# Loading wq as four loads of every fourth partition, in a one-token attention and MLP kernel

## The chip, the cores and the metric

The kernel runs on one core of a Trainium2 chip. The core has five instruction streams: TensorE (PE), VectorE (DVE), ScalarE (ACT), GpSimd (POOL) and SyncE (SP). SP computes nothing; it issues transfers (DMAs), which sixteen DMA engines carry out. The metric is device time in microseconds of one execution. Streams are ordered among themselves by semaphores only: an instruction raises one when it is done, another waits until it has reached a value. A DMA raises its semaphore by 16 when all of its data has landed.

## The reference

One token of width 1024 goes through attention over a window of cached keys and values, and through an MLP; both results are added to the token.

```
xn  = layernorm(x)                                   # x: 1 x 1024
q   = xn @ wq                                        # wq: 1024 x 4096, 32 heads of 128
k,v = last 4096 positions of the caches              # 4 kv heads, each serves 8 q heads
o   = softmax(q k^T / sqrt(128)) v
h   = gelu(layernorm(xn) @ w1 + b1)                  # w1: 1024 x 3584
out = x + o @ wo + h @ w2 + b2                       # wo: 4096 x 1024, w2: 3584 x 1024
```

All arrays are bfloat16. Of work there is little; of weights and cache there are 39.8 MB: wq 8.4, K 4.2, V 4.2, w1 7.3, w2 7.3, wo 8.4.

## The kernel before, in words

Each large array is spread over the 128 partitions of SBUF, so that one partition holds a run of consecutive rows of the weights. For wq that is 8 rows of 4096 numbers: partition p holds rows 8p to 8p+7, which stand in one piece of 64 KB in memory, and in one piece in the tile `WA`.

The order of the loads is written out by hand, in the order in which SP issues them:

- wq into `WA` at the very start (L167, through `load_rows`, whose `dma_start` is L158), one load with semaphore `s_wq[0]`;
- after POOL has built its constants (L200), K into `KT` (L201), w1 into `W1` (L202) and V into `V` (L203), all without a further wait;
- w2 into `WA`, over wq, when the q product is done (L272 and L273);
- wo in six loads into `W1` and `KT`, over w1 and K, when the h product is done (L374 to L379);
- at the end the output (L519).

ACT issues three small loads on a queue of its own: x (L183), b1 (L184), b2 (L238).

On the engines: DVE transposes x and normalizes it with the help of one small matmul (L234 to L253), which gives `XNTb`; a second normalization gives `YTb` for the MLP. PE then forms the q product in `wide_product` (L274 to L287): it waits once for each chunk of weights, here for the single chunk of wq, and runs 64 matmuls of 512 columns (L282). q is brought into the shape that the scores need (L295 to L319). DVE transposes K in place in four parts (L324), PE computes scores (L335), DVE and ACT the softmax (L342 to L370). PE computes the h product with w1 by the same `wide_product` (L373), then the product with V (L426), then the output products with w2 and wo (L456, L463), adding x and b2 on the way. Two additions (L516) and the output's load end the kernel.

Of the kernel before, what the change touches and what calls it, by code (L numbers as in the profile page):

```python
# [19 lines left out]
NQ = 4096  # L20
# [4 lines left out]
WQ_CHUNKS = [8]  # L25
# [22 lines left out]
def bass_parallel_sum__sliding_block_cached__mixer_channel_mlp__decode_kernel(  # L48
# [18 lines left out]
    pe, dve, act, pool, sp = nc.tensor, nc.vector, nc.scalar, nc.gpsimd, nc.sync  # L67

    def sems(name, n):
        return [nc.alloc_semaphore(f"{name}{i}") for i in range(n)]  # L70

    s_x, s_b1, s_b2, s_out = (nc.alloc_semaphore(n) for n in ("s_x", "s_b1", "s_b2", "s_out"))
    s_wq = sems("s_wq", len(WQ_CHUNKS))
# [11 lines left out]
    def sb(name, shape, d):  # L85
        return nc.alloc_sbuf_tensor(name, shape, d)

    f32, bf16 = dt.float32, dt.bfloat16
    WA = sb("WA", [128, KC * NQ], bf16)
# [57 lines left out]
    wq_p = A_wq.rearrange("(p r) n -> p r n", r=KC)  # L147
# [8 lines left out]
    def load_rows(dst, src, chunks, width, semaphores, first=0, c0=0, off=0):  # L156
        for j, n in enumerate(chunks):
            sp.dma_start(  # L158
                dst[:, off + c0 * width: off + (c0 + n) * width].rearrange("p (c n) -> p c n", c=n),
                src[:, first + c0: first + c0 + n, :],  # L160
            ).then_inc(semaphores[j], 16)
            c0 += n
# [1 line left out]
    def load_cache(dst, src, sem):  # L164
        sp.dma_start(dst[:, :], src[0, :, SK - W:SK, :].rearrange("g (m b) d -> m g (b d)", m=32)).then_inc(sem, 16)

    load_rows(WA, wq_p, WQ_CHUNKS, NQ, s_wq)  # L167
    def d(ins):
        return DVE.mark(ins)

# [103 lines left out]
    def wide_product(weights, chunks, width, semaphores, vec, n, banks, name):  # L274
        k = 0
        for j, rows in enumerate(chunks):
            pe.wait_ge(semaphores[j], 16)
            for _ in range(rows):
                for b in range(2):
                    for a in range(4):  # L280
                        lo = k * width + (2 * a + b) * n
                        last = pe.matmul(  # L282
                            PS[32 * a:32 * a + 32, banks[b] * 512: banks[b] * 512 + n],
                            lhsT=vec[:, k:k + 1].to_broadcast([128, 32]), rhs=weights[:, lo:lo + n],
                            start=(k == 0), stop=(k == KC - 1))
                k += 1
        C[name] = PE.mark(last)  # L287

    wide_product(WA, WQ_CHUNKS, NQ, s_wq, XNTb, 512, [4, 5], "q")

    sp.wait_ge(PE.sem, C["q"])
# [79 lines left out]

    pe.wait_ge(ACT.sem, C["exp0"])
    wide_product(W1, W1_CHUNKS, F, s_w1, YTb, QW // 2, [4, 5], "h")  # L373
    sp.wait_ge(PE.sem, C["h"])  # L374
    load_rows(W1, wo_p, WO_CHUNKS[:2], D, s_wo[:2])
# [101 lines left out]
    for a in range(4):  # L477
        q = a % 2
# [25 lines left out]
    for a in range(4):  # L504
        q = a // 2
# [45 lines left out]
```

## Time and profile before

| | us |
|---|---|
| median of three runs | 101.5 (101.06 to 101.81) |
| the profiled execution | 100.91 |
| its span, first to last instruction | 99.5 |
| PE, DVE, ACT, POOL busy | 53.7, 42.0, 10.6, 6.4 |
| moved by DMA | 39.89 MB, 401 GB/s over the span |
| wq: issue to landing | 0.81 to 22.8 |
| K: issue to landing | 5.47 to 32.45 |
| w2: issue to landing | 27.79 to 77.3 |
| wo's largest load: issue to landing | 63.9 to 87.1 |

The profile is one execution, a little shorter than the median run. In its lines L282 is line 282 of the kernel; `out<-in` names the tiles; SPq and ACTq are instructions that issue a DMA. The time of such an instruction is the time to issue, not to move the data; the time to landing stands apart. A line of the timeline is: start, duration, engine, line, operation, tiles, and in brackets how long the engine had been idle and what released it. The chain that ended last is followed back from the last instruction, at each step to what released it. A load in the chain counts from its issue, with all of the time in which it stood in a queue. In the slices each digit is the busy share of one fortieth of the span, in tenths.

### The profile page before, as it was taken

The page shows a single profiled execution, that of the slowest core. Times are in us where ns is not written, and L with a number is a line of the kernel's source. Part 1 is how long each engine was busy: PE and PEld are TensorE (multiplying, and loading weights), DVE is VectorE, ACT ScalarE, POOL GpSimd, SP SyncE. Part 2 cuts the span into 40 slices and gives each one's busy share as a digit, 9 for nine tenths or more (in the row PEclk, how much of TensorE's full clock was granted, in tenths as well). Part 3 has the DMA queues.
Part 4 walks back from the last instruction along what each step waited for, and adds up shares of the span by engine and source line. Part 5 has one row for each costly group of instructions (what it writes and reads, how often), then busy time and mean ns, then how long its engine had stood idle before and what let it go on. Part 6 is the DMA issues. An engine that isn't in the chain of part 4 may idle for free.

```text
span 99.5 us, 859 instructions
## 1 busy us (share of the span) xinstructions
PE 53.7 (54%) x355; PEld 20.0 (20%) x355; DVE 42.0 (42%) x49; ACT 10.6 (11%) x21; POOL 6.4 (6%) x26
## 2 busy tenths in 40 slices
PE   0000220008912019999690359709999299997770
PEld 0000220003400002222120224204344033442220
DVE  0000443000073999999999202999600620000022
ACT  0000336000022000000000297000000000000030
POOL 6773000000000000000000000000000000000000
PEclk9999999999999555557999755885579957999999
DMA  9399999959999888998699999998889999999920
GB/s 369 158 448 448 503 528 422 448 250 435 421 421 580 369 369 369 484 622 352 273 435 474 421 451 392 484 599 369 369 369 431 421 421 415 412 430 387 394 90 1
DMA packets 1622, 39.89 MB, mean 401 GB/s; under 512 B 200, under 2 KB 468, under 8 KB 596
## 3 DMA queue, kind: packets, MB, share of 16 engines
q1 hardware_dynamic: 1596, 39.85, 93.7%
q8 instruction: 2, 0.03, 0.1%
q10 hardware_dynamic: 24, 0.01, 0.0%
HBM read 39.86 MB, written 0.00 MB: 401 GB/s over the span
## 4 chain that ended last, share of the span: by engine, by line
DMA 58%; DVE 22%; PE 10%; POOL 4%; ACT 2%; issue 2%; SPq 1%; POOLq 0%; DVEq 0%
DMA KT<-in_A_wo_dram 31%; DMA KT<-in_A_k_cache_dram 27%; DVE KT L324 18%; PE PS L282 6%; DVE MX L344 2%; PE PS L335 2%; ACT WA L366 1%; PE PS L456 1%; POOL B1R L180 1%; DVE BULK L509 1%; ACT Q L348 1%; SPq L158 1%; PE PS L360 1%; POOL QB L189 1%; DVE ORow L516 0%
## 5 line engine op out<-in xcount | busy, mean ns | idle before, releaser
L324 DVE STREAM_TRANSPOSE KT<-KT 128x4096 bf16<-128x4096 bf16 x4 | 17.4, 4415 | 1.3 <-DMA KT<-in_A_k_cache_dram 1.3
L335 PE MATMUL PS<-KT,QB 128*128 128x512 bf16 x32 | 11.7, 504 | 6.4 <-DVE KT L324 6.4
L426 PE MATMUL PS<-V,WA 128*128 128x512 bf16 x32 | 9.7, 479 | 0.0
L282 PE MATMUL PS<-WA,XNTb 128*32 128x512 bf16 x64 | 4.9, 478 | 8.0 <-DMA WA<-in_A_wq_dram 8.0
L456 PE MATMUL PS<-WA,GT 128*1 128x512 bf16 x56 | 7.9, 451 | 0.0
L509 DVE COPY BULK<-PS 1x256 f32<-1x256 f32 x2 | 0.8, 414 | 15.6 <-PE PS L456 15.5
L245 PE MATMUL PS<-XT,onesf 128*128 128x16 f32 x2 | 0.6, 384 | 11.5 <-DVE XT L242 11.5
L456 PE MATMUL PS<-W,OT 128*1 128x512 bf16 x50 | 5.7, 379 | 1.1 <-DMA W<-in_A_wo_dram 1.1
L282 PE MATMUL PS<-W,YTb 128*32 128x448 bf16 x64 | 5.5, 530 | 1.5 <-ACT WA L366 1.5
L295 DVE CAST Q<-PS 128x512 bf16<-128x512 f32 x1 | 0.7, 692 | 11.7 <-PE PS L282 11.7
L335 PEld LDWEIGHTS PS<-KT,QB 128*128 128x128 bf16 x32 | 3.0, 113 | 12.2 <-DVE KT L324 7.5
L234 DVE STREAM_TRANSPOSE XT<-XB 128x256 bf16<-128x256 bf16 x1 | 0.6, 626 | 10.4 <-DMA XB<-in_A_x_dram 10.4
L426 PEld LDWEIGHTS PS<-V,WA 128*128 128x128 bf16 x32 | 3.7, 119 | 5.6 <-issue 3.5
L370 DVE STREAM_TRANSPOSE WA<-WA 128x4096 bf16<-128x4096 bf16 x1 | 4.4, 4434 | 0.0
L331 PE MATMUL PS<-MRow,ML 4*128 4x512 bf16 x8 | 3.8, 469 | 0.7 <-DVE QB L317 0.7
L282 PEld LDWEIGHTS PS<-WA,XNTb 128*32 128x32 bf16 x64 | 1.9, 118 | 10.6 <-DMA WA<-in_A_wq_dram 8.2
L366 ACT ACTIVATE WA<-PS,NMB 128x1024 bf16<-128x1024 f32 (+2 forms) x3 | 3.7, 1252 | 1.8 <-DVE NMB L362 1.8
L456 PEld LDWEIGHTS PS<-WA,GT 128*1 128x1 bf16 x56 | 2.8, 96 | 4.7 <-issue 2.5
L511 ACT ACTIVATE BULK<-PS 1x256 f32<-1x256 f32 x2 | 0.7, 374 | 25.5 <-PE PS L456 25.4
L434 DVE TENSOR_TENSOR HW<-PS,MG 128x512 f32<-128x512 f32 x1 | 0.7, 692 | 6.0 <-PE PS L426 6.0
L282 PEld LDWEIGHTS PS<-W,YTb 128*32 128x32 bf16 x64 | 2.3, 138 | 4.3 <-issue 2.5
L348 ACT ACTIVATE Q<-PS 128x512 f32<-128x512 f32 x1 | 0.6, 597 | 23.5 <-DVE MX L344 23.5
(98 smaller groups left out, 42.0 us busy)
## 6 DMA issues: line engine op xcount, KB each, us to landing
W<-in_B_w_dram SPq DMA_DIRECT2D x1, 7168.0 KB, 44.5
WA<-in_B_w_dram SPq DMA_DIRECT2D x1, 7168.0 KB, 49.5
KT<-in_A_k_cache_dram SPq DMA_DIRECT2D x1, 4096.0 KB, 27.0
V<-in_A_v_cache_dram SPq DMA_DIRECT2D x1, 4096.0 KB, 53.6
W<-in_A_wo_dram SPq DMA_DIRECT2D x1, 4096.0 KB, 23.2
W<-in_A_wo_dram SPq DMA_DIRECT2D x1, 2304.0 KB, 28.3
KT<-in_A_wo_dram SPq DMA_DIRECT2D x1, 1024.0 KB, 30.4
KT<-in_A_wo_dram SPq DMA_DIRECT2D x1, 512.0 KB, 31.2
```

What stands on the lines that cost most here:

```text
L158: sp.dma_start(dst[:, off + c0 * width: off + (c0 + n) * width].rearrange("p (c n) -> p c n", c=n), src[:, first + c0: first + c0 + n, :], ...
L282: last = pe.matmul(PS[32 * a:32 * a + 32, banks[b] * 512: banks[b] * 512 + n], lhsT=vec[:, k:k + 1].to_broadcast([128, 32]), rhs=weights[: ...
L324: C["kt"].append(d(dve.transpose(KT[:, j * W:(j + 1) * W], KT[:, j * W:(j + 1) * W])))
L331: pe.matmul(bank(nb), lhsT=ML[:, :], rhs=MRow[:, :].unsqueeze(1).to_broadcast([4, 16, 32]), start=True, stop=False)
L335: last = pe.matmul(bank(nb), lhsT=QB[:, c * 128:(c + 1) * 128], rhs=kg[:, c, 16 * nb:16 * nb + 16, :], start=False, stop=(c == 3))
L344: C["mx1"] = d(dve.tensor_reduce(out=MX[:, 1:2], in_=PS[:, 2048:4096], axis=AX.X, op=ALU.max))
L348: C["s7"] = ACT.mark(act.activation(out=S7, in_=bank(7), func=ACTF.Copy))
L366: C[f"exp{j}"] = C["exp"] = ACT.mark(act.activation(out=PT[:, lo:lo + n], in_=src, func=ACTF.Exp, bias=NMB[:, 0:1], scale=SCALE, accum_out ...
L370: C["PT"] = d(dve.transpose(PT, PT))
L426: last = pe.matmul(bank(3), lhsT=PT[:, t * 128:(t + 1) * 128], rhs=V[:, t * 512:(t + 1) * 512], start=(t == 0), stop=(t == 31))
L456: ins = pe.matmul(PS[32 * q:32 * q + 1, 6 * 512:7 * 512], lhsT=vec[:, c:c + 1], rhs=row[:, :, q * 256:(q + 1) * 256], start=first, stop=last)
L509: d(dve.tensor_copy(dst, src))
```

## The change

wq comes in four loads. Load i takes the partitions i, i+4, i+8 and so on, 32 of them with their 64 KB each, and all four raise the same semaphore. PE waits for the sum of the four, 64, ahead of the q product; for the h product it waits for 16 as before. Nothing else differs; the lines of the changed kernel stand one further down.

```
-    load_rows(WA, wq_p, WQ_CHUNKS, NQ, s_wq)
+    for i in range(4):
+        sp.dma_start(WA[i:128:4, :], wq_p[i:128:4, :, :].rearrange("p r n -> p (r n)")).then_inc(s_wq[0], 16)
...
-            pe.wait_ge(semaphores[j], 16)
+            pe.wait_ge(semaphores[j], 64 if name == "q" else 16)
```

## The prediction

> **What bounds the kernel now.** I read the chain that ended last first, in order of time. Its two long pieces are waits for a transfer:
>
> ```profile
> 5.47 26.98 DMA KT<-in_A_k_cache_dram
> 32.47 17.44 DVE KT L324 x4
> ...
> 64.73 30.41 DMA KT<-in_A_wo_dram
> 95.14 0.04 issue
> 95.19 1.05 PE PS L456 x8
> ```
>
> A load of 1 MB that takes 30.41 us is not moving for 30 us; it stands in a queue. So the next view is the page's slices, with the queues:
>
> ```profile
> DMA  9399999959999888998699999998889999999920
> ...
> DMA packets 1622, 39.89 MB, mean 401 GB/s; under 512 B 200, under 2 KB 468, under 8 KB 596
> ...
> q1 hardware_dynamic: 1596, 39.85, 93.7%
> ```
>
> SP's queue, q1, carries all but some hundredths of a MB and fills 93.7% of the sixteen DMA engines' span. The two weak slices (a 3 and a 5) are no idle time: a packet is booked where it starts, and wq's packets are 64 KB. The packet records of the trace show each engine taking eight packets of 64 KB for wq, the first starting between 1.82 and 2.69 us, each later one in 2.42 us and right behind the one before it; the eighth ends between 21.8 and 22.4 us. From there to the last weights no engine pauses, apart from two fetches of instructions of about 1 us, each on a single engine.
>
> Next, SP's own instructions, to see who can delay that stream:
>
> ```profile
> 0.81 0.38 SPq L158 DMA_DIRECT2D WA<-in_A_wq_dram  x1
> 5.47 0.63 SPq L165 DMA_DIRECT2D KT<-in_A_k_cache_dram  x1
> 6.14 0.58 SPq L158 DMA_DIRECT2D W<-in_B_w_dram  x1
> 6.77 0.55 SPq L165 DMA_DIRECT2D V<-in_A_v_cache_dram  x1
> 27.79 0.34 SPq L158 DMA_DIRECT2D WA<-in_B_w_dram  x1
> 63.89 0.80 SPq L158 DMA_DIRECT2D W<-in_A_wo_dram  x2
> ```
>
> Landing is issue plus the page's time to landing. K lands at 32.45, w1 at 50.6, V at 60.4, w2 at 77.3, and the chain's last load at 95.14. w2 is issued at 27.79, 32 us before the queue in front of it is empty (V's landing). wo is issued at 63.89, 13 us before w2 has landed. So neither the q product nor the score and softmax chain decides the end: **a change of wq counts by how much it shifts the DMA stream**, and compute has 13 us to spare against it.
>
> Last, what waits for wq itself:
>
> ```profile
> 10.45 0.63 DVE L234 STREAM_TRANSPOSE XT<-XB 128x256 bf16<-128x256 bf16 x1 [10.45 <-DMA XB<-in_A_x_dram]
> 13.37 0.29 DVE L253 TENSOR_SCALAR XNTb<-XT,msx 128x8 bf16<-128x8 f32 x1
> 22.81 4.93 PE L282 MATMUL PS<-WA,XNTb 128*32 128x512 bf16 x64 [8.04 <-DMA WA<-in_A_wq_dram]
> ```
>
> The normalized x is ready at 13.66 us; the q product starts at 22.81, when the whole of wq is there.
>
> **The change part by part.** The sum is made against the profiled execution: 100.91 us, of which 99.5 are span and 1.4 lie around it. The three runs shown have a median of 101.5, 0.6 above it, so what comes out is put on that median.
>
> *The wait (L277, 64 in place of 16).* Still one wait ahead of the first matmul, for all of wq. No matmul may start early and none is held longer; queued behind it on PE is the same q product. Cost 0.
>
> *What moves.* The same 128 rows of 64 KB, 8.4 MB. Load i takes rows i, i+4, ..., two rows for each of 16 engines if the rows are dealt out evenly. Whether they are dealt so that sixteen engines still run side by side isn't shown for 32 rows. The nearest rows are the K and V loads: the outermost dimension of their source counts 32 too (m in L165), and their 32 KB packets took 1.213 us, which is 27.0 GB/s an engine, as for wq (64 KB in 2.42 us, 27.1). I take 0; the other end is the third rival.
>
> *The issue.* One instruction becomes four. A load of 128 plain rows took SP 0.34 to 0.43 us (0.38 for wq); loads of other shapes took 0.50 to 0.68 (b2 0.50, V 0.55, K 0.63, out 0.68). I take 0.55 for a load of every fourth partition, by V, which also stands behind other loads. Four take 2.2 us, 0.81 to about 3.0. K is held at 5.47 by POOL's constants (SP waits 4.5 us for them), so K, w1 and V leave when they did. If POOL's cover were gone, K would leave some 1.8 us later and still have 16 us of wq in front of it. The engines need the second load only after two packets each, at about 6.7 us, when all four are issued. So only the first issue counts: first packets come 1.01 us after wq's issue starts, 0.63 after it ends; 0.55 in place of 0.38 shifts them by **+0.17** (bounds: 0.34 gives -0.04, 0.68 gives +0.30).
>
> *The start of the engines.* First packets start over 0.87 us and mostly take about 3.0, not 2.42. If that comes from 128 rows being written out for sixteen engines, 32 rows would go quicker. If all sixteen started at 1.82 and ran at once at full rate, first packets would end at 4.24 in place of a typical 5.11: **-0.87**. But two engines that start at 1.82 and 2.37 end their first packet together at 4.86; ends don't follow starts. I take a small share, -0.1, and keep 0 and -0.87 as ends.
>
> *The seams.* There are three more ends of a load. One seam is in the trace: wq's last packet, a 4-byte semaphore write of 0.009 us, then K's first packet; K's landing is 9.68 us behind wq's, and eight packets of 1.213 us are 9.70. A seam costs about 0.01, three **+0.03** (upper end: the full latency of an isolated load, out's 1.7 us from issue to landing, three times, 5.1).
>
> [...]
>
> *The x load.* x, b1 and b2 go by ACT's queue, and the packet records show x's 512 bytes waiting for wq's second packet to end. Three more loads at SP while ACT issues x (2.06, 1.07 us long) may hold x back by a packet or two, 2.42 us each. The 9.1 us between 13.66 and 22.81 hide up to three; without that cover the q product would slip, and the 13 us of wo's issue are behind it. Cost 0.
>
> Sum: +0.17 - 0.1 + 0.03 = +0.1. **101.0 for the profiled execution, 101.6 on the median.** By the bounds of the first two terms the sum lies between -0.9 and +0.4.
>
> **The rivals.**
> 1. *An earlier start.* The small first load reaches the engines sooner and the slow first packets go: down to -0.9 us, 100.6, and more if the issue gets shorter too. For it: the 0.87 us spread. Against it: the ends that don't follow the starts, and a first issue of another shape.
> 2. *The seams cost (slower).* Engines drain at each end of a load before they go on. Place: three seams, at two packets' distance; price 0.35 us each if the next packet waits until the last one's semaphore has arrived (21.8 to 22.16 in the records), +1.1, to 5.1 by a full latency: 102.6 to 106.6. It decides as soon as a seam is over 0.35. Against it: the seam from wq to K.
> [...]
>
> [...]
>
> **How the numbers follow.** About 1% (1.0 us) is what a measurement of this kernel can tell from no change; the three runs alone span 0.75. Chances: the forecast 0.72; rival 1 0.12 (two thirds of it over 1%); rival 2 0.09; rival 3 0.07. That gives faster 0.08, same 0.76, slower 0.16. The range leaves out rival 3, most of rival 2 and the far part of rival 1: from 100.6 (the bound of -0.9) to 102.6 (a seam of 0.35).
>
> **What would show it.** In the changed profile: four issues on SP of about 0.55 us from 0.81, K's still at 5.47. wq's last landing and the start of the q product at 22.8 within half a microsecond; K 9.7 us behind; the chain again ending in a wo load that waits in the queue. Right steps with a wrong size: the q product's start and the end move by the same amount. Rival 1: both earlier by 0.5 to 1. Rival 2: wq 1 to 5 us later with packets still of 2.42 us. [...] Wrong altogether: an end that moves while K's landing doesn't.

## The result, and the profile after

The changed kernel takes 101.33 us (median of 22 runs, 101.03 to 101.98) against 100.84 before (22 runs): the ratio is 1.0054, with a 95% interval of 1.0039 to 1.007. That is half a microsecond more: real, and inside the 1% that the prediction called no change. Forecast was +0.1 us; 0.39 to 0.71 us are measured. Ratios and mean spans here and below leave out the few runs that were over 1.5% above the fastest of their kernel. The forecast time, 101.6 us, lies nearer to 101.33 than its terms deserve, and that is luck: it stood on a median of three runs, 101.5, which is 0.66 us above that of 22 runs, and this made up for the 0.39 us by which the sum fell short.

The timeline of SP's queue after, to hold against the one before (start, duration, issue):

```profile
0.81 2.72 SPq L168 DMA_DIRECT2D WA<-in_A_wq_dram  x4
5.45 0.58 SPq L165 DMA_DIRECT2D KT<-in_A_k_cache_dram  x1
6.09 0.61 SPq L158 DMA_DIRECT2D W<-in_B_w_dram  x1
6.74 0.55 SPq L165 DMA_DIRECT2D V<-in_A_v_cache_dram  x1
28.77 0.33 SPq L158 DMA_DIRECT2D WA<-in_B_w_dram  x1
65.85 0.81 SPq L158 DMA_DIRECT2D W<-in_A_wo_dram  x2
```

One issue of 0.38 us has become four, 2.72 us from the first to the last; the trace's records of the single ones give 0.58, 0.57, 0.59 and 0.84. K, w1 and V still leave at 5.45 to 6.74, behind POOL's constants. The timeline of the engines shows what became of x and of the q product:

```profile
8.65 0.63 DVE L235 STREAM_TRANSPOSE XT<-XB 128x256 bf16<-128x256 bf16 x1 [8.65 <-DMA XB<-in_A_x_dram]
11.57 0.29 DVE L254 TENSOR_SCALAR XNTb<-XT,msx 128x8 bf16<-128x8 f32 x1
23.16 5.56 PE L283 MATMUL PS<-WA,XNTb 128*32 128x512 bf16 x64 [10.20 <-DMA WA<-in_A_wq_dram]
```

x is there 1.80 us earlier (8.65 in place of 10.45), and that buys nothing: the q product waits for wq as before, 10.2 us now, and starts 0.35 later (23.16 in place of 22.81). The chain that ended last, its long pieces:

```profile
5.45 27.39 DMA KT<-in_A_k_cache_dram
32.87 17.43 DVE KT L325 x4
...
66.70 28.81 DMA KT<-in_A_wo_dram
95.51 0.04 issue
95.56 1.04 PE PS L457 x8
```

K lands 0.40 us later (32.85, before 32.45), the 1 MB load of wo 0.37 later (95.51, before 95.14), and the span is 0.4 longer. In this pair of profiles the offset that wq picks up at the start runs through the whole stream and comes out at the end nearly unchanged (0.35, 0.40, 0.37). On the way wo is issued 1.96 us later (65.85 in place of 63.89), mostly because the score matmuls behind K's last part took 4.2 us in place of 2.3, at a granted clock of 0.52 of full speed in place of 1.00. Its landing doesn't move with it: wo only waits a little less in the queue (28.81 in place of 30.41). That is the 13 us of cover, seen at work.

Where the offset comes from stands in the packet records, read for the sixteen first packets of wq in both traces:

| | before | after |
|---|---|---|
| first issue, start and duration | 0.81, 0.38 | 0.81, 0.58 |
| first packet starts at | 1.82 | 2.17 |
| from the end of the issue to it | 0.63 | 0.78 |
| sixteen first packets, median duration | 3.06 | 3.22 |
| the other 112 packets, median | 2.42 | 2.42 |
| wq landed | 22.77 | 23.12 |

### The profile page after: what moved, and what is told of

The parts are those of the page before. It is cut to its first block, busy times and chain, and to the rows that moved or that the text cites. A ratio compares the mean times of both kernels' runs of the same rounds, so it can differ in the third digit from the quotient of the medians.

```text
span 99.9 us, 862 instructions
## 1 busy us (share of the span) xinstructions
PE 53.8 (54%) x355; PEld 19.9 (20%) x355; DVE 42.0 (42%) x49; ACT 10.6 (11%) x21; POOL 6.4 (6%) x26
## 4 chain that ended last, share of the span: by engine, by line
DMA 56%; DVE 22%; PE 12%; POOL 4%; ACT 2%; issue 2%; SPq 1%; POOLq 0%; DVEq 0%
DMA KT<-in_A_wo_dram 29%; DMA KT<-in_A_k_cache_dram 27%; DVE KT L325 17%; PE PS L283 5%; PE PS L336 4%; DVE MX L345 2%; ACT WA L367 1%; PE PS L457 1%; POOL B1R L181 1%; DVE BULK L510 1%; ACT Q L349 1%; SPq L158 1%; PE PS L361 1%; PE PS L332 1%; POOL QB L190 1%
## 5 line engine op out<-in xcount | busy, mean ns | idle before, releaser
L283 PE MATMUL PS<-WA,XNTb 128*32 128x512 bf16 x64 | 5.6, 524 | 10.2 <-DMA WA<-in_A_wq_dram 10.2
L345 DVE TENSOR_REDUCE MX<-PS 128x1 f32<-128x2048 f32 x1 | 2.3, 2292 | 2.0 <-PE PS L336 2.0
```

Source lines behind the costliest of these rows:

```text
L283: last = pe.matmul(PS[32 * a:32 * a + 32, banks[b] * 512: banks[b] * 512 + n], lhsT=vec[:, k:k + 1].to_broadcast([128, 32]), rhs=weights[: ...
L345: C["mx1"] = d(dve.tensor_reduce(out=MX[:, 1:2], in_=PS[:, 2048:4096], axis=AX.X, op=ALU.max))
```

## The experiments

The theory after these two traces: a load of every fourth partition is handed over in a more general form than a plain load of 128 rows; its issue is longer by 0.20 us, its first packet follows 0.15 us later still, and as nothing else is in the queue at that moment all sixteen engines stand idle for 0.35 us more. The rival: it is the four loads, with their seams or their small shares of two rows an engine. Ratios below are to the kernel before on the same chip, with 95% intervals.

**One load, general form.** A switch of the builder keeps the load off the short form; rows, partitions and the number of loads stay.

```
+    nc.dge_precook = False
     load_rows(WA, wq_p, WQ_CHUNKS, NQ, s_wq)
+    nc.dge_precook = True
```

> One load of all 128 partitions as in the kernel before, but handed to SP in the general form that loads of other shapes take, not in the short form of a plain load of 128 rows. Theory (the form of the first issue is the whole cost): issue of wq 0.6 to 0.7 us in place of 0.38, first packets and wq's landing 0.3 to 0.4 us later, time like the changed kernel's, ratio 1.003 to 1.006. Rival (it is the four loads, by their seams or by the small share of an engine in each): issue of another length but the time of the kernel before, ratio 1.000 within 0.0015.

Measured: 101.23 us, ratio 1.0042 (1.0011 to 1.0072), and on SP's queue:

```profile
0.81 0.58 SPq L158 DMA_DIRECT2D WA<-in_A_wq_dram  x1
5.47 0.57 SPq L165 DMA_DIRECT2D KT<-in_A_k_cache_dram  x1
```

The issue takes 0.58 as in the changed kernel (0.38 without the switch), the first packet starts at 2.17 as there, and in the runs the loss is there with a single load: the interval leaves out a ratio of 1. The profile alone would not have shown it. Expected were a landing of wq 0.3 to 0.4 us later and an issue of at least 0.6; wq landed only 0.17 later than before (22.94), because the last of its first packets ended only 0.16 later (5.64, before 5.48), and the profile's span is 99.55 us, before 99.52.

**Four plain loads.** Two of each partition's eight rows in each load, all 128 partitions, one wait for 64.

```
-    load_rows(WA, wq_p, WQ_CHUNKS, NQ, s_wq)
+    load_rows(WA, wq_p, [2, 2, 2, 2], NQ, s_wq * 4)
```

> Four loads of two rows of wq each, all 128 partitions, 16 KB a partition, plain shape, one wait for 64. Theory (form of the first issue): wq's first issue 0.35 to 0.4 us, time of the kernel before, ratio 1.000 within 0.0015; wq's landing at 22.8 within 0.15. Rival (seams): three seams as in the changed kernel, ratio 1.003 to 1.006.

Measured: 100.79 us, ratio 0.9997 (0.9975 to 1.0018). SP's queue:

```profile
0.81 1.87 SPq L158 DMA_DIRECT2D WA<-in_A_wq_dram  x4
5.47 0.62 SPq L165 DMA_DIRECT2D KT<-in_A_k_cache_dram  x1
```

The first of the four took 0.38, the first packet started at 1.82, wq landed at 22.87. Four loads with three seams cost nothing that can be measured (at most 0.18 us by the interval), so the seams aren't the cause. This run also tells on the earlier start: its first packets are 16 KB and end between 2.64 and 3.56, and yet wq lands no earlier. The start of the stream is slow with small packets too (the sixteen first ones took 1.17 us in the median, later ones 0.61), so loads of fewer bytes at the start gained nothing here.

**Plain first.** One row of each partition as a plain load, the other seven by every fourth partition; the wait, left out in the lines below, is for 80.

```
+    load_rows(WA, wq_p, [1], NQ, s_wq)
     for i in range(4):
-        sp.dma_start(WA[i:128:4, :], wq_p[i:128:4, :, :].rearrange(...)).then_inc(s_wq[0], 16)
+        sp.dma_start(WA[i:128:4, NQ:], wq_p[i:128:4, 1:, :].rearrange(...)).then_inc(s_wq[0], 16)
```

> wq's first row of each partition (8 KB) as one plain load of 128 partitions, then the other seven rows as four loads of every fourth partition. Theory (only the first issue counts): five loads, four seams, four issues of 0.65 us, and still the time of the kernel before, ratio 1.000 within 0.002, for the later issues are hidden behind 2.4 us of the first load. Rival (general form or seams wherever they stand): ratio 1.004 or more.

Measured: 100.83 us, ratio 1.0 (0.9976 to 1.0024).

```profile
0.81 0.39 SPq L158 DMA_DIRECT2D WA<-in_A_wq_dram  x1
1.26 2.48 SPq L169 DMA_DIRECT2D WA<-in_A_wq_dram  x4
```

Four general issues of 0.55 to 0.63 us are all there, and the loss is gone: from 1.84 us on the engines have packets to move while the issues go on. Here it was the issue ahead of an empty queue that counted: one general issue of 0.58 us there gave 1.0042, four behind a plain load 1.0.

**All loads in the general form.** The switch of the first experiment, left off for the whole kernel.

> The kernel before with every load in the general form. Theory (only an issue ahead of an empty queue counts): w1, w2 and wo each take 0.2 to 0.3 us longer to issue, some 2 us over the kernel, but only wq's first issue is seen, ratio 1.003 to 1.006 as with wq alone. Rival (each issue is on the path): about 2 us, ratio 1.015 to 1.025.

Measured: 101.11 us, ratio 1.0028 (1.0007 to 1.0049), no more than with wq alone (just under the 1.003 that was expected at least). SP's queue, wq's issue and the late loads:

```profile
0.81 0.55 SPq L158 DMA_DIRECT2D WA<-in_A_wq_dram  x1
...
28.79 0.47 SPq L158 DMA_DIRECT2D WA<-in_B_w_dram  x1
65.69 1.12 SPq L158 DMA_DIRECT2D W<-in_A_wo_dram  x2
66.84 1.25 SPq L158 DMA_DIRECT2D KT<-in_A_wo_dram  x2
68.14 1.25 SPq L379 DMA_DIRECT2D KT<-in_A_wo_dram  x2
```

In the profile before, the last two of these lines were

```profile
64.73 0.94 SPq L158 DMA_DIRECT2D KT<-in_A_wo_dram  x2
65.72 0.92 SPq L378 DMA_DIRECT2D KT<-in_A_wo_dram  x2
```

The first packet starts at 2.15, as in the other runs that begin with this form. The seven late issues take 4.09 us in place of 3.00 in the profile before. I had expected about 2 us over the kernel, and it is 1.1 (w1's issue, 0.58 before, took 0.60 and hardly changed); none of it is seen in the time: w2 is issued at 28.79, before V has landed (60.4), and wo from 65.69 to 69.39, before w2 has landed (77.4), so that the queue ahead of each is not empty.

**Two loads of every second partition.** The loop over 2 with a step of 2, a wait for 32.

> Two loads of every second partition, 64 each. Theory (form of the first issue, whatever the number of rows): first issue 0.55 to 0.6 us, first packet 0.3 to 0.4 us later than before, ratio 1.003 to 1.006. Rival (part of the cost goes with the number of loads): about half of the changed kernel's loss, ratio 1.002 to 1.003.

Measured: 101.11 us, ratio 1.0054 (1.0027 to 1.008). First issue 0.58, first packet at 2.17, wq landed at 23.10, all as with four loads. Half of the loss would have been 1.0027, the interval's very end, so this speaks for a cost by the form and not by the number, less sharply than the four plain loads do.

**A small load ahead of wq.** The kernel before, and ahead of wq one load of four rows of 512 bytes, into a tile that nothing reads (the tile, its semaphore and a wait for it at the very end are left out in the lines below).

```
+        sp.dma_start(EXTRA[0:128:32, :], b2_rows).then_inc(s_extra, 16)
     load_rows(WA, wq_p, WQ_CHUNKS, NQ, s_wq)
```

> The kernel before with one small load more (four rows of 512 bytes, into a tile that nothing reads) issued by SP ahead of wq, so that wq's issue, still of the short form, starts later. Theory (each delay of the stream's start reaches the end in full): wq's issue starts 0.55 to 0.7 us later, time plus 0.5 to 0.7 us, ratio 1.005 to 1.007. Rival (the start has slack, the changed kernel's loss has another cause): ratio 1.000 to 1.002.

Measured: 101.56 us, ratio 1.008 (1.0061 to 1.0099).

```profile
0.81 0.69 SPq L170 DMA_DIRECT2D EXTRA<-in_B_b_dram  x1
1.56 0.38 SPq L158 DMA_DIRECT2D WA<-in_A_wq_dram  x1
```

The extra issue took longer than I had allowed, so wq's starts 0.75 us later; its first packet is 0.76 later (2.58) and the runs are 0.8% longer, 0.6 to 1.0 us. Within that interval, what delays the start of the stream comes out at the end in full.

**The changed kernel again,** on the chip of the last two.

> The changed kernel unaltered, beside the others on the same chip. Expected: ratio 1.004 to 1.006 as before; a ratio above that of one load in the general form (1.0042) by more than their intervals would say that the four loads cost something beyond the first issue.

Measured: 101.10 us, ratio 1.0051 (1.0032 to 1.007). It overlaps widely with the single load in the general form, so no cost of the four loads beyond the first issue shows.

**Contiguous quarters.** Load i takes partitions 32i to 32i+31.

```
-        sp.dma_start(WA[i:128:4, :], wq_p[i:128:4, :, :].rearrange(...)).then_inc(s_wq[0], 16)
+        sp.dma_start(WA[32 * i:32 * i + 32, :], wq_p[32 * i:32 * i + 32, :, :].rearrange(...)).then_inc(s_wq[0], 16)
```

> The changed kernel with partitions 32i to 32i+31 in load i in place of every fourth. [...] Rival (which partitions a load takes makes no difference): time of the changed kernel, 101.3 us.

Measured: 121.81 us, ratio 1.2109 (1.2077 to 1.2141). SP's queue and the q product, from two stretches of the timeline, and the slices of the page (GB/s, each slice 3.0 us):

```profile
0.82 1.94 SPq L168 DMA_DIRECT2D WA<-in_A_wq_dram  x4
5.47 0.63 SPq L165 DMA_DIRECT2D KT<-in_A_k_cache_dram  x1
```

```profile
44.07 1.04 PE L283 MATMUL PS<-WA,XNTb 128*32 128x512 bf16 x8 [26.17 <-DMA WA<-in_A_wq_dram]
```

```profile
GB/s 348 0 348 153 196 350 0 349 109 239 348 0 348 33 326 511 348 479 609 305 419 495 310 479 381 479 435 514 324 590 305 432 402 435 435 383 402 412 209 2
```

The issues are short here (the first 0.40), and the first packet starts at 1.86; the data itself is slow. wq lands at 44.03 in place of 22.77, and from the fifteenth slice on, once K follows, the slices are back near the old rate. In the packet records wq's packets of 64 KB take 5.11 us, a little over twice the 2.42 of the kernel before. The author's estimate for this run, at most twice 2.42, was 4.84 us a packet, a landing of wq at 38 to 42 us and a time of 116 to 121 us; all three came out above it. The zeros among the slices are no pauses: a packet is booked where it starts, and one of 5.11 us reaches beyond its slice of 3.0. wq's 8.4 MB in 42.2 us, from first packet to landing, are 199 GB/s. So which partitions a load takes is what decides here, 21 us of it: loads of every fourth and of every second partition ran at 2.42 us a packet. Why the contiguous quarters run at half the rate is not shown.

**The delay of the start against the span, over all runs.** One profile is a thin witness for a third of a microsecond. In the profiles of one load and of all loads in the general form the 1 MB load of wo lands only 0.03 and 0.05 us later than before. Of this load's sixteen semaphore increments (sixteen 4-byte writes in the packet records) 14 had come by 93.75 us in the profile before, and the last two at 95.07 and 95.14. Those two are probably the engines that each took one of the two fetches of instructions (1.02 and 1.06 us in the records, from 46.6 and 83.9), so that the end of one profile tells of two engines and not of sixteen. The mean span of the runs, first to last instruction, is the better measure. Against the kernel before on the same chip, with intervals of 0.09 to 0.16 us to either side:

| run | first packet later, one profile | mean span longer |
|---|---|---|
| four plain loads | 0.00 | 0.05 |
| plain first | 0.02 | 0.00 |
| all loads in the general form | 0.33 | 0.35 |
| one load, general form | 0.35 | 0.37 |
| two loads of every second partition | 0.35 | 0.36 |
| the changed kernel again | 0.36 | 0.43 |
| a small load ahead of wq | 0.76 | 0.81 |

In all seven the span grows by what the first packet is late, within these intervals.

None of these versions is faster than the kernel before: the plain forms are equal to it, and the others are slower.

## Why the prediction was right, point by point

*The bound.* Right, and shown: delays of the stream's start of 0.35 and 0.76 us came out at the end (ratios 1.0054 and 1.008), while wo's issue 1.96 us later, x 1.80 us earlier and 1.1 us more of late issues did not. It is the case that the prediction calls right steps with a wrong size: the q product's start moved by 0.35 us and the end by 0.37.

*The wait (0).* Right as far as the trace tells: one wait, released by wq's last landing.

*What moves (0).* Right: 112 packets at 2.42 us in both kernels. The reason given, K's source counting 32, was thin; the contiguous quarters also load 32 rows each and go at half the rate. What kept the rate is the step of four between partitions (2.42 us a packet, 5.11 without it). Rival 3, with 0.07 among the chances, was the author's estimate of packets at twice 2.42 us, 4.84, and a time of 120.9. In the changed kernel the 2.42 excludes it; in the contiguous quarters a loss of that size is real, 5.11 us a packet and 121.81 us in time, but no run shows what halves the rate.

*The issue (+0.17).* This is the term that was mis-sized. 0.55 was taken for the issue and 0.58 measured, a small miss. But the prediction held the 0.63 us from the end of an issue to the first packet for fixed, and for this form it is 0.78 or 0.79 in every run in which wq began with it: the changed kernel and its repetition, every second partition, one load, all general. 0.20 and 0.15 make +0.35, just beyond the upper bound of +0.30. By its bounds the whole sum reaches +0.33, not the +0.4 stated, and the measured 0.49 us lies above it. No row of the trace before had shown the longer gap: the output's transfer, the only other one ahead of an empty queue, has its first packet 0.60 us after the end of its issue. The fault was to carry the 0.63 over to another form without bounds. Two rows were also read too neatly: w1 is a plain load like wq and took 0.58 us, and one of wo's plain loads 0.47, outside the 0.34 to 0.43 that were given for that kind; and b2's 0.50 is an issue of ACT, not of SP. So an issue's length depends on more than the form, and only for the first issue do the runs separate the two (0.38 to 0.40 plain, 0.55 to 0.58 general).

*The start of the engines (-0.1).* Wrong in its sign at most: the median first packet took 3.22 and, in the repetition, 3.16 us against 3.06, and 16 KB packets brought wq no sooner. A first load of 32 rows in the plain form (the contiguous quarters) had its first packet at 1.86, where 128 rows had theirs at 1.82. Rival 1 is excluded with it.

*The seams (+0.03).* Right within what can be measured: four plain loads gave 0.9997 (0.9975 to 1.0018), and in the changed kernel's own trace the semaphore writes at its seams take 0.009 us each. Rival 2, with 1.1 us or more, is excluded: the interval of the four plain loads leaves at most 0.18 us for three seams.

*The x load (0).* The time was right, the direction wrong: x was feared late and came 1.80 us early. The last of its four semaphore writes of 4 bytes started 0.03 us after the last of its data, at the seam (8.10 and 8.08 us), where before it had waited behind another 64 KB packet (10.09 and 7.65).

+0.35 is what one trace shows; the whole times say 0.39 to 0.71, and the mean spans of the four versions that begin with this form 0.35 to 0.43. So the delay of the first packet is nearly all of it. What is left is of the size by which the first packets differ from profile to profile (medians of 3.06 to 3.22 us), and stays open. Why the longer form costs 0.20 and 0.15 us stays open too.

## What to carry to other kernels

In this kernel the transfer queue is full from the first load to the last, and what counted was its beginning and its rate: a first packet 0.33 to 0.36 us late made the span 0.35 to 0.43 us longer, and wq's packets at 5.11 us in place of 2.42 made the time 21 us longer. In such a kernel the first load should be the one that is issued and started quickest (here 0.38 us and 0.63 to the first packet, against 0.55 to 0.58 and 0.78 or 0.79), and what stands behind it may be issued more slowly as long as the queue ahead of it stays full (1.1 us more was not seen here). Splitting a load that stands in a full queue was free here (a ratio of 0.9997 for four plain loads); the partitions that each part takes were not (1.2109 for contiguous quarters), so keep each part spread as the steps of two and four were, and compare packet times before and after. A cost that looks like "four instead of one" can be the first of the four alone: undo number and form separately.

## What the runs showed of the hardware that was not expected

- As the first issue, a load of every fourth or second partition costs SP 0.58 us where a plain one costs 0.38 to 0.40, and its first packet follows the end of the issue after 0.78 us in place of 0.63. The first of the contiguous quarters of 32 partitions was issued in 0.40, so the step between partitions makes the difference there, not their number. The gap is not the same for every load that is not plain: it was 0.74 us for the small load ahead of wq and 0.60 for the output.
- wq's first packets, on an idle queue, were slow in both sizes: 64 KB took 3.06 us (median) where later ones took 2.42, 16 KB took 1.17 where later ones took 0.61. wq landed within 0.1 us of the same time in both cases.
- Contiguous quarters of 32 partitions ran at less than half the rate: 5.11 us a packet, where twice 2.42 would be 4.84, and 121.81 us in time against 101.10 for every fourth partition on the same chip.
